# Attention's last units and the entry to the experts: rows turned later, both early gathers together, last logits on VectorE, last x on ScalarE, third expert's rows gathered early

## Chip, cores and metric

The kernel runs on one core of a Trainium2 chip. The metric is device time in microseconds (us) of one launch. Engines are named as in the profile: PE (TensorE matmul), DVE (VectorE), ACT (ScalarE), POOL (GpSimd), SP (SyncE, which here issues loads and stores).

## The reference

Attention without softmax, a norm, then a mixture of experts in which each row goes to one expert or to none:

```python
kv = np.einsum('bhsd,bhse->bhde', k, v)          # B=8, H=8, S=576, D=64
out = np.einsum('bhsd,bhde->bhse', q, kv)
rms = np.sqrt(np.mean(out * out, axis=-1, keepdims=True) + 1e-06)
attn = out / rms * g_norm
x = attn.transpose(0, 2, 1, 3).reshape(4608, 512)
do_compute = x @ w_skip > 0                       # rows that get an expert
logits = x[do_compute] @ w_gate                   # 8 experts
e_idx = np.argmax(logits, axis=1)
gate_w = softmax(logits)[range(len(logits)), e_idx]
h = np.maximum(x[rows_of_e] @ w1[e], 0.0)         # 512 -> 1024
y[rows_of_e] = gate_w * (h @ w2[e])               # 1024 -> 512
out = x;  out[do_compute] = x[do_compute] + y
```

## The kernel before

**Order.** The order of the program text is the order on each engine: it is written by hand. Attention is cut into 36 units n = 0 to 35 (NU = 36), each of 128 positions of two tiles and half the heads; the units of one tile pair are a couple, u = 0 and u = 1. The last couple, 34 and 35, holds the positions that don't fill a tile (i is None) of several batches.

**One turn of the attention loop** (L951 to L984), for n from 0 to 37: PE turns q of unit n+1; ACT takes the square root for n-1 (root, L525); jobs booked as "early"; PE multiplies q by the state (values, L496, or L504 for units 34 and 35) and ACT squares the product (L510); jobs "mid"; DVE sums the squares (squares, L518; from n = 30 ahead of norm) and for n-1 takes the reciprocal (L532) and multiplies the PSUM product by it into xl (norm, L537, 128x584: per head 64 values of x and 9 partial logits, eight experts and the skip score); jobs "pe"; POOL adds the partial logits (finish: lp L554 for each unit, lp+lp L558 and lg L562 for each couple); jobs "dve"; jobs "end". The product with g that makes x itself (xb, L567, on POOL) is kept in a list and issued one unit later by scale(), behind that unit's reciprocal; from the couple's second xb a store to the output follows. Units 30 and 33 hold their product in the PSUM tile sum_ps, all others in one of two tiles o_ps.

**The choice of experts** goes in three groups, when units 12, 22 and 36 are done (ends). choose (L608 to L634, DVE): mx, sh, oh, fi, fi, ohb, of which ohb marks each row's expert. rank (PE, L645 to L651): counts the rows of each expert up to every row. number (DVE, L662 to L677): turns the counts into a place for each row, lo_i and hi_k, and the one-hot oha. hits and weighed (L690 ohc, L698 bv) and place (PE, L710) then bring each row's number to its place: settle is place for a group of tiles.

**The early start.** After the second group, early() (L842 to L883) finds expert 0's first 192 rows from what is known by then: a small one-hot, place (L869), rows (L873), row and src (L859, L861), then a POOL gather of 128 rows (L863) and, booked as a job of the same turn, put_more: a matmul (L879), row and src, a gather of 64 rows. first_in(0) and first_in(1) turn the gathered rows on PE (L801) and ACT copies them to xt_first (L828, L830); first_layer_1 (L814) makes the first IN = 2 of the FC = 8 slices of layer 1, ACT their relu into ht_first (L817).

**At n = 36**: DVE makes ohc of the known groups (128x528), then choose of the last group; scale(NU, chosen[-1]) issues the last three xb (units 33, 34, 35) behind ohb; then bv for the known groups (L698).

**Entry to the experts** (L1484 to L1507, quoted in the diff). layer_1 makes slices of layer 1 for expert 0's first rows (L1112, relu on ACT L1114 into ht0), layer_2 slices of layer 2 for one piece of them (L1124), again_rows and slot_rows (L1051) the tables of row numbers (src, asrc for reading, rows, arows for writing), gather_all(r) the gathers of expert r (L1084, on POOL), gates() the softmax weights, expert_in turns gathered rows (L1093, ACT copies to xt). Expert 0's remaining rows then go through layer 1 (L1112 on xt). From expert 1 on the products are done in the fast form of L1192, with ACT copying intermediate sums p and u (L1202) and DVE adding (L1196). In experts(), gather_all(2) stands in the turn of r = 0 (L1423), and later experts' gathers two turns ahead. The results are scaled on DVE (L1336) and scattered to the output by POOL (L1339).

Of the kernel before, what the change touches and what calls it, by code (L numbers as in the profile page):

```python
# [8 lines left out]
FP32 = mybir.dt.float32  # L9
# [3 lines left out]
ALU = mybir.AluOpType  # L13
# [4 lines left out]
def kernel(  # L18
# [423 lines left out]
    def at(step, part, job):  # L442
        todo.setdefault((step, part), []).append(job)
# [84 lines left out]
    def norm(n):  # L528

        nq, b, i, u = units[n]  # L530
        (ps, _), rs = ops.pop(n), rss.pop(n)
        inverse = nc.vector.reciprocal(out=rs[:, :, :], in_=rs[:, :, :])  # L532
        if n < NU - 2:
            scale(n, inverse)
        r4 = rs[:, :, :].unsqueeze(3)
        xl = att_pool.tile([P, 2, 2, PK], FP32, tag="xl", name="xl", bufs=4)
        nc.vector.tensor_tensor(  # L537
            out=xl[:, :, :, :].rearrange("p x y (a k) -> p x (y a) k", a=2),
            in0=ps[:, :, 0:2 * PK].rearrange("p x (h k) -> p x h k", k=KD),
            in1=r4.to_broadcast([P, 2, 4, KD]), op=ALU.mult)  # L540
        return lambda: finish(n, xl)

    def finish(n, xl):
        nq, b, i, u = units[n]
        g = sum(2 * nq >= x for x in ends)
        t0 = 2 * nq - ([0] + ends)[g]
        if t0 == 0 and u == 0:
# [8 lines left out]
        if u == 1:  # L556
            del halves[nq]
            nc.gpsimd.tensor_tensor(out=lp[:, 0, :, :, :], in0=lp[:, 0, :, :, :],  # L558
                                    in1=lp[:, 1, :, :, :], op=ALU.add)
            both = lp[:, 0, :, :, :] if i is not None else \  # L560
                lp[:, 0, :, :, :].rearrange("p r w g -> p w r g")
            nc.gpsimd.tensor_tensor(out=lgs[g][:, t0:t0 + 2, :], in0=both[:, 0, :, :],  # L562
                                    in1=both[:, 1, :, :], op=ALU.add)
        if u == 0:
            xbs[nq] = xb_pool.tile([P, 2, DM], FP32, tag="xb", name="xb")
# [242 lines left out]
    def first_layer_1():  # L808

        hps = ps_q.tile([P, 512], FP32, tag="q", name="q_ps")  # L810
        for f in range(IN):
            cols = slice(f * KEPT, (f + 1) * KEPT)
            for dc in range(DC):
                nc.tensor.matmul(out=hps[:, cols], lhsT=w_sb[0][0][:, dc, f * P:(f + 1) * P],  # L814
                                 rhs=xt_first[:, dc, :], start=(dc == 0), stop=(dc == DC - 1),
                                 skip_group_check=True)
        at(NU, "early", lambda: nc.scalar.activation(  # L817
            out=ht_first[:, :, :], in_=hps[:, 0:IN * KEPT].rearrange("p (f t) -> p f t", f=IN),
# [20 lines left out]
    assert ends[LAST - 1] == 4 * (KNOWN // S) + 2  # L839
    NE = ends[LAST - 1]  # L840

    def early():  # L842
# [24 lines left out]
        def put():  # L867
            for t in range(NE):
                nc.tensor.matmul(out=ps, lhsT=oha_k[:, t, :],  # L869
                                 rhs=bv[:, t, :, :].rearrange("p c i -> p (c i)"), start=(t == 0),  # L870
                                 stop=(t == NE - 1), skip_group_check=True)
            rows = gat_pool.tile([P, 2], FP32, tag="rows1", name="rows1")
            nc.vector.tensor_reduce(out=rows[:, :], in_=ps.rearrange("p (c i) -> p c i", i=2),  # L873
# [3 lines left out]
            def put_more():  # L877
# [3 lines left out]
                gather(more, 64, P)  # L881
            at(now[0], "pe", put_more)
        yield "mid", put  # L883
# [62 lines left out]
    for part in range(2):  # L946
        at(NU - 3 + 2 * part, "early", lambda part=part: first_in(part))
    at(NU - 1, "end", first_layer_1)

    PACE = (2, 4)  # L950
    for n in range(NU + 2):  # L951
# [17 lines left out]
        if n == NU:  # L969
            ohc = hits(0, NE, colid_i, gat_pool, NE)  # L970
            drain(choose(LAST))
            scale(NU, chosen[-1])
            first_bv = weighed(ohc, 0, NE, row_k, 2, gat_pool, NE)
        jobs(n, "dve")
# [16 lines left out]
    with tc.tile_pool(name="wpool_b", bufs=1, reuse_waits="tile") as wpool_b, \  # L991
# [391 lines left out]
        def experts(pieces, widths, srcs, xt, ht, yps0, tables, group):  # L1383

            for r in range(E):
# [36 lines left out]
                if r == 0:  # L1422
                    gather_all(2, pieces, *srcs)  # L1423
                    ys = [bank() for _ in todo]
# [82 lines left out]
        load_ahead(0, landed)  # L1507
# [73 lines left out]
```

## Time and profile before

| | us |
|---|---|
| three runs | 380.49, 382.15, 384.62 (median 382.15) |
| the profiled execution | 381.18 |
| its span, first to last instruction | 379.4 |
| TensorE clock granted, mean | 0.997 of full |

The profile is one execution, cut into instructions by engine. A row of a timeline gives start, duration, engine, line, operation, out<-in with the shape, the count, and in brackets how long the engine had been idle and what ended that. A row of the waits gives the total, the count and the longest. Of the places named above:

| what | line, engine | first start, us | duration, us |
|---|---|---|---|
| gathers of the first rows, 128 and 64 | L863 POOL | 107.39, 109.98 | 1.08, 1.01 |
| turning the first 128 rows | L801 PE | 111.43 | 0.63 |
| values of 33, 34, 35 | L496, L504 PE | 111.89, 112.99, 115.53 | 1.17, 0.74, 0.74 |
| first slices of layer 1 | L814 PE | 116.72 | 2.9 |
| xl of 34, 35 | L537 DVE | 118.12, 119.13 | 0.77 each |
| last logits lg | L562 POOL | 121.04 | 0.22 |
| ohc of the known groups | L690 DVE | 119.82 | 0.70 |
| rank | L645 PE | 123.32 | 0.7 |
| last three xb | L567 POOL | 123.09 | 5.27 together |
| gathers of experts 0 and 1 | L1084 POOL | 134.86 to 141.44 | about 1 each |
| expert 0's remaining rows, layer 1 | L1112 PE | 142.78 | 4.3, twice |
| scatters of expert 0's rows | L1339 POOL | 154.07, 155.40 | about 1 each |
| gathers of expert 2 | L1084 POOL | 163.15, 164.45, 165.73 | about 1 each |

### The profile page before, as it was taken

The page shows a single profiled execution, that of the slowest core. Times are in us where ns is not written, and L with a number is a line of the kernel's source. Part 1 is how long each engine was busy: PE and PEld are TensorE (multiplying, and loading weights), DVE is VectorE, ACT ScalarE, POOL GpSimd, SP SyncE. Part 2 cuts the span into 40 slices and gives each one's busy share as a digit, 9 for nine tenths or more (in the row PEclk, how much of TensorE's full clock was granted, in tenths as well). Part 3 has the DMA queues.
Part 4 walks back from the last instruction along what each step waited for, and adds up shares of the span by engine and source line. Part 5 has one row for each costly group of instructions (what it writes and reads, how often), then busy time and mean ns, then how long its engine had stood idle before and what let it go on. Part 6 is the DMA issues. An engine that isn't in the chain of part 4 may idle for free.

```text
span 379.4 us, 9624 instructions
## 1 busy us (share of the span) xinstructions
PE 363.5 (96%) x3848; PEld 312.1 (82%) x3848; DVE 244.9 (65%) x626; ACT 142.4 (38%) x383; POOL 124.9 (33%) x195
## 2 busy tenths in 40 slices
PE   8999999999988999989999999999999999999994
PEld 4688797898877759669879987988988988998983
DVE  3355457767878861846757656875876876877831
ACT  2466575766763302214402420430440430431410
POOL 7036467555677560234113303212202211202003
PEclk9999999999999999999999999999999999999998
DMA  8999999995669639945716362772662762700001
GB/s 288 394 391 387 402 402 400 404 372 196 189 242 262 184 98 323 387 145 199 250 39 218 127 224 59 244 269 51 235 226 70 263 197 95 269 3 28 29 1 53
DMA packets 32039, 81.70 MB, mean 215 GB/s; under 512 B 2474, under 2 KB 2482, under 8 KB 31988
## 3 DMA queue, kind: packets, MB, share of 16 engines
q1 hardware_dynamic: 28176, 69.47, 52.2%
q0 software_dynamic: 3792, 11.53, 9.1%
q8 instruction: 32, 0.52, 0.6%
q14 instruction: 19, 0.16, 0.1%
q10 hardware_dynamic: 20, 0.02, 0.1%
HBM read 66.80 MB, written 14.48 MB: 214 GB/s over the span
## 4 chain that ended last, share of the span: by engine, by line
PE 81%; issue 9%; ACT 3%; DVE 3%; POOL 2%; DMA 1%; POOLq 0%; DVEq 0%; ACTq 0%
PE bank L1192 44%; PE bank L1124 7%; PE o_ps L496 6%; PE sum_ps L379 5%; PE bank L1112 4%; PE q_ps L460 3%; PE g_ps L393 2%; PE bank L1093 2%; PE q_ps L170 2%; DMA xg<-out_dram,src 1%; DVE rs L518 1%; DVE xl L537 1%; ACT sq L510 1%; PE q_ps L814 1%; PE g_ps L411 1%
## 5 line engine op out<-in xcount | busy, mean ns | idle before, releaser
L1202 ACT COPY p<-bank 128x128 f32<-128x128 f32 (+6 forms) x70 | 20.8, 297 | 102.1 <-PE bank L1192 89.6
L1192 PE MATMUL bank<-xt,w 128*128 128x128 f32 (+5 forms) x336 | 55.5, 288 | 0.3 <-DVE bank L1196 0.3
L567 POOL TENSOR_TENSOR xb<-xl,g_b 128x512 f32<-128x512 f32 x36 | 44.4, 1235 | 32.3 <-DVE rs L532 30.4
L1192 PEld LDWEIGHTS bank<-xt,w 128*128 128x128 f32 x336 | 47.0, 190 | 2.2 <-DVE bank L1196 1.3
L1196 DVE TENSOR_TENSOR bank<-bank,p 128x128 f32<-128x128 f32 (+6 forms) x70 | 23.6, 337 | 37.1 <-PE bank L1192 35.5
L1192 PE MATMUL bank<-xs,s 128*128 128x128 f32 (+5 forms) x224 | 36.9, 289 | 1.6 <-ACT p L1202 1.6
L496 PE MATMUL o_ps<-kvd,qT 128*128 128x146 f32 x240 | 35.8, 290 | 1.0 <-ACT kvd L415 0.7
L1339 POOL DMA_INDIRECT out_dram<-xg,arows x9 | 10.6, 1174 | 74.4 <-DVE xg L1336 68.8
L1124 PE MATMUL bank<-w,ht 128*32 128x128 f32 (+2 forms) x436 | 34.5, 319 | 0.0
L518 DVE TENSOR_REDUCE rs<-sq 128x8 f32<-128x512 f32 x36 | 24.6, 682 | 15.1 <-ACT sq L510 14.9
L1192 PEld LDWEIGHTS bank<-xs,s 128*128 128x128 f32 x224 | 31.1, 190 | 2.7 <-ACT p L1202 2.6
L496 PEld LDWEIGHTS o_ps<-kvd,qT 128*128 128x128 f32 x240 | 31.6, 188 | 2.0 <-ACT kvd L415 1.5
L1339 POOL DMA_INDIRECT out_dram<-xg,rows x14 | 13.9, 994 | 55.6 <-DVE xg L1336 54.3
L1124 PEld LDWEIGHTS bank<-w,ht 128*32 128x32 f32 (+2 forms) x436 | 18.8, 120 | 13.2 <-issue 10.9
L537 DVE TENSOR_TENSOR xl<-o_ps,rs 128x584 f32<-128x584 f32 x34 | 26.1, 767 | 4.5 <-DVE rs L532 0.5
L1084 POOL DMA_INDIRECT xg<-out_dram,src x14 | 14.5, 1038 | 39.7 <-DMA out_dram<-xg,rows 13.4
L1192 PE MATMUL bank<-t,ht 128*128 128x256 f32 x112 | 27.1, 385 | 0.0
L1192 PE MATMUL bank<-w,ht 128*128 128x256 f32 x112 | 27.1, 384 | 0.0
L510 ACT ACTIVATE sq<-o_ps 128x512 f32<-128x512 f32 x34 | 20.3, 596 | 15.0 <-PE o_ps L496 14.4
L1192 PE MATMUL bank<-t,hs 128*128 128x256 f32 x112 | 25.3, 379 | 0.0
L379 PE MATMUL sum_ps<-v,k 64*64 64x64 f32 x1152 | 24.7, 223 | 0.4 <-issue 0.4
L379 PEld LDWEIGHTS sum_ps<-v,k 64*64 64x64 f32 x1152 | 20.8, 134 | 4.3 <-issue 1.9
(217 smaller groups left out, 679.5 us busy)
## 6 DMA issues: line engine op xcount, KB each, us to landing
w<-in_moe_w_dram SPq DMA_DIRECT2D x16, 2048.0 KB, 9.8
k<-in_k_dram SPq DMA_DIRECT2D x16, 576.0 KB, 9.9
v<-in_v_dram SPq DMA_DIRECT2D x16, 576.0 KB, 10.6
q<-in_q_dram SPq DMA_DIRECT2D x16, 576.0 KB, 11.2
out_dram<-xb SPq DMA_DIRECT2D x29, 256.0 KB, 8.9
out_dram<-xb POOLq DMA_DIRECT2D x7, 256.0 KB, 5.9
xg<-out_dram,src POOLq DMA_INDIRECT x16, 3.4
out_dram<-xg,rows POOLq DMA_INDIRECT x16, 6.9
```

The costliest lines, as they stand in the source:

```text
L379: nc.tensor.matmul(out=sum_ps[w * 64:(w + 1) * 64, a, u, :], lhsT=kt[r, 2 * u + w, c, :], rhs=vt[r, 2 * u + w, c, :], start=(c == 0), stop ...
L496: nc.tensor.matmul(out=ps[:, w, 0:2 * PK].rearrange("p (r k) -> p r k", r=2)[:, :, cols], lhsT=qT[:, w, a, :], rhs=kvds[b % KVD][:, u, w, ...
L510: nc.scalar.activation(out=sq[:, :, :, :], in_=heads(ps, G, G + 2 * D), func=ACT.Square)
L518: nc.vector.tensor_reduce(out=rs[:, :, :], in_=sq[:, :, :, :].rearrange("p x y (a d) -> p x (y a) d", a=2), axis=AX.X, op=ALU.add)
L537: nc.vector.tensor_tensor(out=xl[:, :, :, :].rearrange("p x y (a k) -> p x (y a) k", a=2), in0=ps[:, :, 0:2 * PK].rearrange("p x (h k) -> ...
L567: late.append((lambda: nc.gpsimd.tensor_tensor(out=xb[:, :, 4 * u * D:(4 * u + 4) * D].rearrange("p r (w x) -> p r w x", w=2), in0=xl[:, : ...
L1112: nc.tensor.matmul(out=hps[:, cols], lhsT=w_sb[r][0][:, dc, f * P:(f + 1) * P], rhs=xt[:, dc, cols], start=(dc == 0), stop=(dc == DC - 1))
L1124: nc.tensor.matmul(out=yps[q * m:(q + 1) * m, 0:n], lhsT=ht(f)[:, off:off + m], rhs=w_sb[r][1][:, f, q * n:(q + 1) * n], start=(f == 0), s ...
L1192: nc.tensor.matmul(out=out, lhsT=lhsT(i), rhs=rhs(i), start=start and i == 0, stop=i == k - 1, skip_group_check=True)
L1196: nc.vector.tensor_tensor(out=to, in0=x, in1=y, op=ALU.add)
L1202: nc.scalar.copy(out=t, in_=x)
L1339: ins = nc.gpsimd.indirect_dma_start(out=cut_rows(m)[:, :], out_offset=bass.IndirectOffsetOnAxis(ap=rows[:, col:col + 1], axis=0), in_=x, ...
```

## The change

1. first_in(0) moves from the "early" jobs of turn 33 (ahead of values(33)) to its "pe" jobs (behind it).
2. put_more runs directly after the first gather, so that the two gathers stand together on POOL. ohc of the known groups is made in early() rather than at n = 36.
3. For units 34 and 35, DVE makes no xl. last_logits multiplies only the logits' 36 + 36 columns by the reciprocal (two instructions a unit) and, after 35, one reduction over the eight heads gives lg; POOL's lp, lp, lp+lp and lg for this couple are gone. last_x: ACT makes x, 16 copies of 128x64 with the reciprocal as a scale. They are issued at n = 36, behind root(35), and the relu L817 behind them. The xb of 33 is issued one turn earlier (scale for n < NU-1); those of 34 and 35 wait for ACT, no longer for ohb.
4. At the entry, one slice of layer 1 (f = 2) stands ahead of rank instead of three; the others fill the places between the tables; layer 2's first slices come after them; all three experts' gathers (nine, before six) are issued together, and r = 0 issues none.

```diff
@@ norm, finish
-        if n < NU - 2:
+        if n < NU - 1:
             scale(n, inverse)
         r4 = rs[:, :, :].unsqueeze(3)
         xl = att_pool.tile([P, 2, 2, PK], FP32, tag="xl", name="xl", bufs=4)
+        if n >= NU - 2:
+            last_logits(n, ps, rs)
+            last_x.append(lambda: norm_by_scalar(n, ps, rs, xl))
+            return None
...
+    def last_logits(n, ps, rs):
+        nq, b, i, u = units[n]
+        if u == 0:
+            halves[nq] = att_pool.tile([P, 2, G, 8], FP32, tag="le", name="le", bufs=1)
+        le = halves[nq]
+        for a in range(2):
+            nc.vector.tensor_tensor(
+                out=le[:, :, :, 4 * u + a:4 * u + a + 3:2].rearrange("p r g w -> p r w g"),
+                in0=ends_of(heads(ps, 0, PK))[:, :, :, a, :],
+                in1=rs[:, :, a:a + 3:2].unsqueeze(3).to_broadcast([P, 2, 2, G]), op=ALU.mult)
+        if u == 1:
+            g, t0 = place_of_logits(nq)
+            nc.vector.tensor_reduce(out=lgs[g][:, t0:t0 + 2, :], in_=halves.pop(nq)[:, :, :, :],
+                                    axis=AX.X, op=ALU.add)
+
+    def norm_by_scalar(n, ps, rs, xl):
+        for r in range(2):
+            for h in range(4):
+                w, a = divmod(h, 2)
+                cols = slice(G + a * D, G + (a + 1) * D)
+                nc.scalar.activation(out=xl[:, r, w, cols],
+                                     in_=heads(ps, cols.start, cols.stop)[:, r, w, :],
+                                     func=ACT.Copy, scale=rs[:, r, h:h + 1])
+        weigh(n, xl)
@@ first_layer_1
-        at(NU, "early", lambda: nc.scalar.activation(
+        at(NU, "dve", lambda: nc.scalar.activation(
@@ early
+            known_at.append(hits(0, NE, colid_i, gat_pool, NE))
             rows = gat_pool.tile([P, 2], FP32, tag="rows1", name="rows1")
...
-            at(now[0], "pe", put_more)
+            put_more()
@@ jobs
-        at(NU - 3 + 2 * part, "early", lambda part=part: first_in(part))
+        at(*((NU - 3, "pe"), (NU - 1, "early"))[part], lambda part=part: first_in(part))
@@ the loop
         if n == NU:
-            ohc = hits(0, NE, colid_i, gat_pool, NE)
+            for job in last_x:
+                job()
+            scale(NU)
             drain(choose(LAST))
-            scale(NU, chosen[-1])
-            first_bv = weighed(ohc, 0, NE, row_k, 2, gat_pool, NE)
+            first_bv = weighed(known_at[0], 0, NE, row_k, 2, gat_pool, NE)
@@ experts, r == 0
-                    gather_all(2, pieces, *srcs)
+                    if yps0 is None:
+                        gather_all(2, pieces, *srcs)
@@ entry
-        layer_1(0, xt_first, ht0, slice(0, KEPT), range(IN, 5))
+        layer_1(0, xt_first, ht0, slice(0, KEPT), range(IN, 3))
         rank(LAST)
         drain(number(LAST))
-        layer_1(0, xt_first, ht0, slice(0, KEPT), range(5, FC))
+        layer_1(0, xt_first, ht0, slice(0, KEPT), range(3, 4))
         settle(0, NE, first_bv)
         last_bv = columns(NE, NT - NE, colid_i, row_k, 2, gat_pool, NE)
-        y, y_more = [layer_2(0, ht_of, piece, None, range(IN)) for piece in first]
+        layer_1(0, xt_first, ht0, slice(0, KEPT), range(4, 7))
         settle(NE, NT, last_bv)
-        layer_2(0, ht_of, first[0], y, range(IN, 3))
+        layer_1(0, xt_first, ht0, slice(0, KEPT), range(7, FC))
         arows = slot_pool.tile([P, NRES], I32, tag="arows", name="arows")
         asrc = slot_pool.tile([P, NRES], I32, tag="asrc", name="asrc")
         again_rows(arows, asrc, range(0, SOON))
         rows, src = slot_rows(slice(0, NCOL), slot_pool, "")
-        layer_2(0, ht_of, first[0], y, range(3, 4))
+        y, y_more = [layer_2(0, ht_of, piece, None, range(IN)) for piece in first]
         again_rows(arows, asrc, range(SOON, len(runs)))
-        layer_2(0, ht_of, first[0], y, range(4, FC))
-        for r in range(2):
+        for r in range(3):
             gather_all(r, plan, src, asrc)
+        layer_2(0, ht_of, first[0], y, range(IN, FC))
         gates()
-        layer_2(0, ht_of, first[1], y_more, range(IN, 5))
         for piece in plan[0]:
             landed = expert_in(xg0, xt0, piece)
-        yps0 = [y, layer_2(0, ht_of, first[1], y_more, range(5, FC))]
+        yps0 = [y, layer_2(0, ht_of, first[1], y_more, range(IN, FC))]
         load_ahead(0, landed)
```

More of the change, by code (lines that the diff above doesn't have):

```diff
@@ L541, in norm, with place_of_logits @@
         return lambda: finish(n, xl)
+    last_x = []
+    def place_of_logits(nq):
+        g = sum(2 * nq >= x for x in ends)
+        return g, 2 * nq - ([0] + ends)[g]
+    def last_logits(n, ps, rs):
+        nq, b, i, u = units[n]
+        assert i is None
+        if u == 0:
[19 more added lines that the diff above has]
+        weigh(n, xl)
     def finish(n, xl):
         nq, b, i, u = units[n]
-        g = sum(2 * nq >= x for x in ends)
-        t0 = 2 * nq - ([0] + ends)[g]
+        g, t0 = place_of_logits(nq)
         if t0 == 0 and u == 0:
@@ L563, in finish, with weigh @@
                                     in1=both[:, 1, :, :], op=ALU.add)
+        weigh(n, xl)
+    def weigh(n, xl):
+        nq, b, i, u = units[n]
         if u == 0:
@@ L840 @@
     NE = ends[LAST - 1]
+    known_at = []
     def early():
```

## The prediction

> **What bounds the kernel now.** I read the busy table first, then the waits of TensorE (PE) alone, then the timelines of the four engines around the change. The page gives PE 96% of the span:
>
> ```profile
> PE 363.5 (96%) x3848; PEld 312.1 (82%) x3848; DVE 244.9 (65%) x626; ACT 142.4 (38%) x383; POOL 124.9 (33%) x195
> ```
>
> So an edit pays only if it closes one of PE's gaps, and costs if it opens one. The waits of PE, from 90 us to the end, are few (line waited at, what it waited for, us):
>
> ```profile
> PE bank L1192 <- ACT p L1202: 1.6, 1, 1.6
> PE o_ps L504 <- DVE xl L537: 1.4, 1, 1.4
> PE q_ps L801 <- DMA xg<-out_dram,src: 1.2, 1, 1.2
> PE bank L1112 <- issue: 0.6, 1, 0.6
> PE q_ps L814 <- ACT xt_first L830: 0.4, 1, 0.4
> PE g_ps L879 <- DVE rows L873: 0.3, 1, 0.3
> ```
>
> They sum to 5.5 us, all between 105 and 168 us: that is the whole prize. The three that the edits aim at are the gather wait at 111.43 (L801, first rows), the xl wait at 115.53 (L504, unit 35), and the 1.56 us at 167.16 (L1192), which coincides with the third expert's gathers (163.15 to 166.73). After 168 us PE never waits a tenth of a microsecond that this view lists.
>
> The hand-over from attention to experts is on VectorE (DVE) and GpSimd (POOL):
>
> ```profile
> 121.30 0.27 DVE L614 TENSOR_REDUCE mx<-lg 128x14 f32<-128x112 f32 x1 [0.78 <-POOL lg L562]
> ...
> 122.73 0.27 DVE L634 TENSOR_TENSOR ohb<-eorder,fi 128x112 bf16<-128x112 f32 x1
> ```
>
> The last logits come from POOL at 121.26, the choice of experts (mx to ohb) takes 1.7 us, and PE's rank needs ohb at 123.0. PE doesn't notice: three slices of layer 1 lie ahead of rank and run until 123.3.
>
> ```profile
> 119.42 4.06 PE L1112 MATMUL bank<-xt_first,w 128*128 128x192 f32 x24
> ```
>
> **What the Trainium skill says.** "SBUF — State Buffer", section "Who interferes with whom": a DVE instruction with two SBUF inputs and a POOL instruction that reads SBUF exclude each other for a whole instruction; reductions and operations with a PSUM input don't. The trace agrees: src (L861) takes 0.86 us beside an xb (other times 0.16), each oha (L677) 2.03 beside the last xb, and those xb, 1.18 alone, take 2.13 and 2.03. "ScalarE: Activation LUTs", section "What ACT_TABLE_LOAD costs", gives an activation about 186 ns + 0.833 ns an element, some 93 ns more for a scale that is a pointer, about 93 ns of which overlaps the next: 64 elements come every 0.24 us, 0.33 without overlap. The trace before has no such form; its nearest (L525, 8 elements) takes 0.30.
>
> **Part 1, first rows turned after values(33).** Four transposes move behind values(33); nothing is added. The 1.16 us wait at L801 goes, but values(33) then waits for what is late next: its PSUM, which the xl of unit 30 reads until 111.29. It starts at about 111.4 instead of 111.89: **0.5 us** earlier, and so the chain behind it (square, squares, root, xl, values(35), L814). The copy to xt_first, on ScalarE (ACT), now lies behind the square of 33; first rows are needed only at L814, four microseconds later.
>
> **Part 2, both early gathers at once; ohc moved.** Same instructions; on POOL the second gather passes one xb (1.18 us), which is later by the gather's 1.3. POOL works without a gap from 111.0 to 120.2, so its backlog ends where it did: lg of unit 33 at 119.56. The 0.70 us ohc goes from the choice to just ahead of rows (L873), where DVE waits 0.85 us for PE's place (L869) as it is: hidden, at worst 0.7 later. The second row and src come before the squares of 31 instead of behind them; DVE waits for PE's L879 some 0.3 there, and gets it back, since src no longer lies beside an xb (0.86 to 0.16). Gain or loss on PE 0, up to 0.7 lost if unit 30's xl slips.
>
> **Part 3, last logits on DVE, last x on ACT.** DVE loses two xl (2 x 0.77) and gains four products of 36 elements (0.2 each, between L773's 0.18 and L617's 0.27) and one reduction (0.27): -1.54 + 0.8 + 0.27 = -0.5 us. POOL loses lp, lp, lp+lp, lg (0.25 + 0.65 + 0.26 + 0.22 = 1.4 us). ACT gains 16 scaled copies: 16 x 0.24 = 3.8 us, 5.3 at 0.33. They begin behind root(35), 117.92 + 0.30 less the 0.5 of part 1 = 117.7; so unit 34's x is there at 119.6 to 120.4, unit 35's at 121.5 to 123.0. The relu L817 and layer 1's relus queue behind; the first reader of their results on PE is layer 2, eight microseconds on.
>
> The last logits are then done on DVE at about 118.8. But mx reads unit 33's logits too, which POOL ends at 119.56: mx starts at 119.6, not 121.3, **1.7 us earlier**. Now the catch. Before, the last three xb were held behind ohb. After, the xb of 33 follows lg(33) at once (119.6 to 120.7), and those of 34 and 35 as soon as ACT delivers. They take turns with the choice, whose sh, oh, second fi and ohb each read two SBUF inputs: sh waits to 120.7 and ends at 121.0; xb(34) to 122.2; oh to 122.5; the first fi, a reduction, beside xb(35), which holds to 123.7; then second fi (0.2) and ohb (0.3): **ohb at 124.2**. If ACT needs 0.33 a copy, xb(35) comes after ohb, which is then at 123.3. With no exclusion at all: 119.6 + 1.7 = 121.3. I take **124.0**, with 121.3 and 124.2 for the range. Behind it, oha no longer meets an xb: 2 x 1.3 instead of 4.03.
>
> **Part 4, entry to the experts.** Only one slice of layer 1 is left ahead of rank. PE: L814 at 116.2 (116.72 - 0.5), 2.7 us for it, 1.3 for f=2: at rank by 120.2. It waits for ohb: 0.2 us to start behind it, so 124.0 + 0.2 - 120.2 = **4.0 us idle**, where before it was none. From there to the first product on expert_in's rows, PE has the same work as before: the stretch from 116.72 to 142.14 (142.78 less its 0.64 of idle) is 25.4, less the 4.0 already done, 21.4. So 124.2 + 21.4 = 145.6, against 142.78: **+2.8 us** (121.3: 142.9, +0.1). Within it, VectorE must not come late: last_bv at 130.9 before, 7.9 behind ohb, now 1.4 sooner thanks to oha, so 6.5; PE gets to it after rank 0.7, f=3 to 6 5.2 and a settle 0.7 = 6.6. Just in time; a miss costs some tenths.
>
> The third expert's three gathers join the first six on POOL (nine at 1.33 us: about 135.6 to 147.5), and the scatters of expert 0's rows, at 154.07 before, follow. PE waits for none of it: the first six are ahead in the queue as before, and layer 2 of the second piece covers their copies.
>
> The stall at 167.16: PE waited for p from ACT, which was itself released only at 166.80, as the r=2 gathers ended; the weight load of SP moved at 166.69 too. The 0.64 at 142.78 coincides with the first six gathers in the same way. Coincidence is all the trace shows. I take it as caused by the gathers being issued there: **-1.6 us**. If not: 0.
>
> **Sum**, against the profiled execution's own time, 381.18 us (span 379.4 and 1.8 around it): +2.8 - 1.6 = +1.2, so 382.4. The part 1 gain is inside the +2.8, since PE waits for ohb whatever it had saved. That execution lies 1.0 below the median of the runs, 382.15; their spread is 4.1. I put the time at **382.6**.
>
> **Rivals.**
> 1. *Forecast*: xb takes turns with the choice, rank waits 3 to 4 us, the late stall goes: +0.3 to +1.4; 381.5 to 383. For it: the exclusion seen at L861, L677 and L567. Chance 0.40.
> 2. *The choice slips through*: mx goes at 119.6 and POOL's xb lose the race or come late; ohb 121.3 to 122.5. L1112 on xt at 142.9 to 144.1, +0.1 to +1.3, less 1.6: -1.5 to -0.3; 379.5 to 381.5. For it: before, bv went ahead of a waiting xb at 122.93. Against: xb(33) is already running when sh comes. Chance 0.27.
> 3. *Slower: PE's wait for ohb at rank, with nothing given back.* Place: rank (L645), from 120.2. Price: 2.8 us on the path at ohb 124.0, 3.0 at 124.2, with the stall at 167 staying (its cause isn't the gathers, or it moves with them). It decides from ohb later than 121.2 if the stall stays, than 122.8 if it goes. 384 to 384.3; to 385.5 if last_bv and the row tables, behind the same ohb, come a further 1.4 late (the time that oha was to save). For it: PE's last gaps are small and the new one is 4 us. Against: oha is freed. Chance 0.25.
> 4. *It doesn't do what it says*: ACT's copies come so late, or the roots behind them, that POOL's and DVE's order shifts and mx still waits to 121. Then ohb at 122.7 to 123, PE idle 2.7, +1.5, less 1.6: 381. Chance 0.08, shared by both sides.
>
> **How the numbers follow.** Case 1 is likeliest; 2 gives the lower end and 3 the upper. The range, **379.5 to 385.5**, holds cases 1, 2 and most of 3. A measurement of this kernel tells about 1%, 3.8 us, from no change, and no case comes to that but the end of 3 with a mishap added: faster by over 1% 0.04 (nearly the whole prize of 5.5 won), within 1% 0.84, slower by over 1% 0.12.
>
> **What would show it.** In the profile after: mx waiting for lg of unit 33 at about 119.6; sh, oh or fi stretched to 1 us or starting behind an xb's end; PE idle before rank (L645) for <- DVE ohb, 3 to 4 us; oha 1.3; L801 without a wait; L1192 <- ACT p gone. I am wrong if rank waits under 1.5 us (case 2), if the wait at L1192 stays (case 3), or if PE waits for p or weights anywhere after 168 us.

## The result, and the profile after

The changed kernel takes 383.88 us (median of 22 runs, 383.18 to 385.29); the kernel before, in the same job, 383.19 us (22 runs, 380.49 to 385.37). The ratio is 1.0027, 95% interval 1.0011 to 1.0043: slower by 0.4 to 1.6 us. The forecast was 382.6 from a median of 382.15, in a range of 379.5 to 385.5.

The profiled execution of the changed kernel has a span of 382.8 us. Its lines are numbered some 40 higher than before: L504 to L541, L614 to L656, L645 to L687, L814 to L856, L1112 to L1157, L1192 to L1237 are the pairs that matter. Place (L869, now L912), the last step on PE ahead of what the change moves, starts at 106.79 us instead of 105.70, so **1.09 us of the difference in span lies ahead of the change** and is taken off wherever a start is compared below. This lead goes with the execution, not with the kernel. Of the 14 profiles of this document, six record TensorE at full clock, to stay, from 4.2 to 5.5 us, and in these place starts at 105.70 to 106.25 us; the other eight record it from 9.3 to 10.9 us, and there place starts at 106.41 to 107.32. Both groups hold kernels with and without the change's parts.

The page's row of PE, and then its waits from 90 us to the end, after (total, times, longest):

```profile
PE 366.9 (96%) x3848; PEld 314.9 (82%) x3848; DVE 244.0 (64%) x629; ACT 145.4 (38%) x399; POOL 120.8 (32%) x191
```
```profile
PE g_ps L690 <- DVE ohb L676: 2.7, 1, 2.7
PE sum_ps L496 <- ACT sq L510: 0.8, 1, 0.8
PE o_ps L504 <- DVE xl L541: 0.8, 1, 0.8
PE q_ps L856 <- ACT xt_first L872: 0.4, 1, 0.4
PE bank L1157 <- issue: 0.4, 1, 0.4
...
PE bank L1237 <- ACT p L1247: 0.2, 1, 0.2
```

PE is busy 3.4 us longer with the same 3848 products (1.3 of it ahead of place, 2.1 between place and the first fast product), and has no less idle time. The gather wait (1.2) is gone, but 0.8 of it comes back one product later, ahead of values(33); the xl wait fell from 1.4 to 0.8. The 1.6 us wait for p at the third group of fast products (L1192) is gone too: the 0.2 that is listed stands elsewhere, at 206.81 us. The same products before and after:

```profile
167.16 0.85 PE L1192 MATMUL bank<-xs,s 128*128 128x172 f32 x4 [1.56 <-ACT p L1202]
```
```profile
169.62 1.41 PE L1237 MATMUL bank<-xs,s 128*128 128x172 f32 x8
```

The largest wait is new, at rank, for ohb. The timeline of VectorE, before and after, shows how ohb became late: mx starts earlier, but three of the instructions behind it take three to four times as long.

```profile
121.60 0.27 DVE L617 TENSOR_TENSOR sh_k<-lg,mx 128x112 f32<-128x112 f32 x1
121.91 0.27 DVE L622 SCALAR_TENSOR_TENSOR oh<-sh_k,eorder 128x112 f32<-128x112 f32 x1
...
122.52 0.18 DVE L630 SCALAR_TENSOR_TENSOR fi<-lg,fi 128x14 f32<-128x14 f32 x1
```
```profile
120.58 0.27 DVE L656 TENSOR_REDUCE mx<-lg 128x14 f32<-128x112 f32 x1 [0.68 <-POOL lg L599]
120.89 0.93 DVE L659 TENSOR_TENSOR sh_k<-lg,mx 128x112 f32<-128x112 f32 x1
121.86 1.14 DVE L664 SCALAR_TENSOR_TENSOR oh<-sh_k,eorder 128x112 f32<-128x112 f32 x1
123.03 0.27 DVE L669 TENSOR_REDUCE fi<-oh 128x14 f32<-128x112 f32 x1
123.33 0.73 DVE L672 SCALAR_TENSOR_TENSOR fi<-lg,fi 128x14 f32<-128x14 f32 x1
124.10 0.27 DVE L676 TENSOR_TENSOR ohb<-eorder,fi 128x112 bf16<-128x112 f32 x1
...
126.28 2.10 DVE L719 TENSOR_TENSOR oha_k<-row_i,lo_i 128x896 bf16<-128x896 int32 x2
```

On POOL, at the same time, the last three xb, and on ACT the copies that feed them:

```profile
120.51 3.53 POOL L609 TENSOR_TENSOR xb<-xl,g_b 128x512 f32<-128x512 f32 x3
```
```profile
119.15 3.38 ACT L576 ACTIVATE xl<-o_ps,rs 128x64 f32<-128x64 f32 x16 [0.30 <-DVE rs L532]
```

The xb run back to back, 1.18 us each, ending at about 121.7, 122.9 and 124.0; sh, oh and fi end at 121.82, 123.00 and 124.06, each just behind one of these ends. The two reductions, mx and the first fi, keep their 0.27. And PE, behind its wait, is slow for a while:

```profile
121.36 0.38 PE L687 MATMUL g_ps<-top,ident 128*128 128x120 f32 x2
124.43 0.21 PE L690 MATMUL g_ps<-ohb,ut 128*128 128x112 bf16 x1 [2.69 <-DVE ohb L676]
...
124.93 2.25 PE L1157 MATMUL bank<-xt_first,w 128*128 128x192 f32 x8
126.97 1.09 PE L752 MATMUL g_ps<-bv,oha_k 128*128 128x48 bf16 x22
```

Eight products of this shape take about 1.5 us elsewhere. The table by stretches says why; its columns are the stretch, its length, busy time and count of PE, PEld, DVE, ACT and POOL, then the granted clock, the DMA share and GB/s:

```profile
125.00:126.00 1.00, 1.00 (x9) 1.00 (x6) 1.00 (x4) 0.00 (x0) 0.00 (x0) 0.81 1.00 406
126.00:127.00 1.00, 1.00 (x5) 0.83 (x5) 0.97 (x4) 0.00 (x0) 0.00 (x0) 0.50 1.02 410
...
128.00:129.00 1.00, 1.00 (x6) 1.00 (x5) 0.97 (x4) 0.00 (x0) 0.00 (x0) 0.50 0.36 127
129.00:130.00 1.00, 1.00 (x8) 1.00 (x8) 0.95 (x2) 0.00 (x0) 0.00 (x0) 0.99 0.02 8
```

For 3.4 us, from 125.6 to 129, TensorE has half its clock. The forecast didn't have this; when it comes is worked out in the last section.

### The profile page after: what moved, and what is told of

The parts are those of the page before. It is cut to its first block, busy times and chain, and to the rows that moved or that the text cites. A ratio compares the mean times of both kernels' runs of the same rounds, so it can differ in the third digit from the quotient of the medians.

```text
span 382.8 us, 9644 instructions
## 1 busy us (share of the span) xinstructions
PE 366.9 (96%) x3848; PEld 314.9 (82%) x3848; DVE 244.0 (64%) x629; ACT 145.4 (38%) x399; POOL 120.8 (32%) x191
## 4 chain that ended last, share of the span: by engine, by line
PE 82%; issue 6%; POOL 4%; DVE 3%; ACT 3%; POOLq 0%; ACTq 0%; DVEq 0%
PE bank L1237 44%; PE bank L1169 9%; PE o_ps L496 6%; PE sum_ps L379 5%; PE bank L1157 4%; PE q_ps L460 3%; POOL xb L609 2%; PE g_ps L393 2%; PE q_ps L170 2%; PE bank L1138 2%; PE g_ps L1096 1%; PE g_ps L411 1%; PE g_ps L752 1%; ACT qT L463 1%; DVE xl L541 1%
## 5 line engine op out<-in xcount | busy, mean ns | idle before, releaser
L1237 PE MATMUL bank<-xt,w 128*128 128x128 f32 (+5 forms) x336 | 55.5, 288 | 0.4 <-DVE bank L1241 0.3
L609 POOL TENSOR_TENSOR xb<-xl,g_b 128x512 f32<-128x512 f32 x36 | 42.7, 1187 | 30.3 <-DVE rs L532 30.3
L1237 PEld LDWEIGHTS bank<-xt,w 128*128 128x128 f32 x336 | 47.0, 190 | 2.3 <-DVE bank L1241 1.5
L1237 PE MATMUL bank<-xs,s 128*128 128x128 f32 (+5 forms) x224 | 36.8, 288 | 0.2 <-ACT p L1247 0.2
L1237 PEld LDWEIGHTS bank<-xs,s 128*128 128x128 f32 x224 | 31.1, 190 | 1.3 <-ACT p L1247 1.2
L541 DVE TENSOR_TENSOR xl<-o_ps,rs 128x584 f32<-128x584 f32 x32 | 24.5, 767 | 4.3 <-DVE rs L532 0.5
L1237 PE MATMUL bank<-t,ht 128*128 128x256 f32 x112 | 27.1, 385 | 0.0
L1237 PE MATMUL bank<-w,ht 128*128 128x256 f32 x112 | 27.1, 384 | 0.0
L1237 PE MATMUL bank<-t,hs 128*128 128x256 f32 x112 | 25.3, 379 | 0.0
```

Of the source, the lines that this page charges most:

```text
L541: nc.vector.tensor_tensor(out=xl[:, :, :, :].rearrange("p x y (a k) -> p x (y a) k", a=2), in0=ps[:, :, 0:2 * PK].rearrange("p x (h k) -> ...
L609: late.append((lambda: nc.gpsimd.tensor_tensor(out=xb[:, :, 4 * u * D:(4 * u + 4) * D].rearrange("p r (w x) -> p r w x", w=2), in0=xl[:, : ...
L1237: nc.tensor.matmul(out=out, lhsT=lhsT(i), rhs=rhs(i), start=start and i == 0, stop=i == k - 1, skip_group_check=True)
```

## The experiments

Two readings of each profile carry most of what follows: **A**, from place to the first fast product (L1192, L1237), which holds attention's end and the entry, and **B**, from there to the end of the span. Rank's start is that of its second product (L690), the first that needs ohb, counted from place. "Half clock" says whether and where the granted clock falls to 0.5 between 100 us and the end of the work. Ratios are to the runs of before in the same job; the jobs ran on different chips, so ratios of different jobs are compared with care. The names "gathers alone" and "best" stand for the kernels of experiment 7.

| kernel | ratio (95%) | A | B | rank from place | half clock |
|---|---|---|---|---|---|
| before | 1 | 58.46 | 215.24 | 17.83 | no |
| before, second profile | 0.9995 (0.9965 to 1.0025) | 60.24 | 215.77 | 19.63 | 117 to 121 |
| changed | 1.0027 (1.0011 to 1.0043) | 62.15 | 213.86 | 17.64 | 125 to 129 |
| changed, again | 1.0076 (1.0054 to 1.0098) | 61.50 | 213.43 | 17.63 | 125 to 129 |
| third rows late | 1.0049 (1.0027 to 1.0072) | 59.93 | 215.15 | 17.62 | no |
| first rows early | 1.0068 (1.0040 to 1.0096) | 59.95 | 213.44 | 17.66 | no |
| wait filled | 1.0016 (1.0000 to 1.0032) | 60.80 | 213.63 | 17.64 | no |
| no slice ahead | 1.0146 (1.0120 to 1.0172) | 62.91 | 213.44 | 17.63 | 125 to 129 |
| last xb held | 0.9984 (0.9970 to 0.9999) | 59.57 | 213.51 | 15.58 | no |
| entry as before | 0.9959 (0.9944 to 0.9975) | 58.86 | 213.52 | 17.64 | no |
| entry as before, again | 0.9937 (0.9918 to 0.9956) | 59.23 | 213.94 | 17.64 | no |
| gathers alone | 0.9997 (0.9979 to 1.0015) | 59.33 | 213.16 | 19.42 | 117 to 121 |
| gathers alone, again | 0.9963 (0.9943 to 0.9983) | 61.02 | 213.48 | 19.50 | 118 to 122 |
| best | 0.9931 (0.9913 to 0.9950) | 58.82 | 213.77 | 17.34 | no |

**1. The entry's order put back.** The order of work on PE behind attention is that of before; the gathers stay together.

```diff
-        layer_1(0, xt_first, ht0, slice(0, KEPT), range(IN, 3))
+        layer_1(0, xt_first, ht0, slice(0, KEPT), range(IN, 5))
         rank(LAST)
         drain(number(LAST))
-        layer_1(0, xt_first, ht0, slice(0, KEPT), range(3, 4))
+        layer_1(0, xt_first, ht0, slice(0, KEPT), range(5, FC))
         settle(0, NE, first_bv)
...
```

> The changed kernel with the entry's order of before (three slices of layer 1 ahead of rank, layer 2's first slices between the two settles), the nine gathers still together. Theory (PE's 2.7 us of waiting at rank for ohb, and the half clock of TensorE from 125 to 129 us that follows it, are what the change costs): the wait at rank falls from 2.7 to about 0.4 us, the granted clock stays 1.00 at 125 to 129, rank starts within 0.2 us of where it does in the changed kernel, the first product on expert 0's remaining rows starts 3.3 to 3.9 us earlier, and the time is 380 to 381 us, ratio to before 0.990 to 0.995. Rival (the wait is hidden or only moves behind VectorE's tables): ratio stays at 1.001 to 1.004.

The timeline of PE in this run:

```profile
120.58 4.06 PE L1157 MATMUL bank<-xt_first,w 128*128 128x192 f32 x24
...
124.96 0.21 PE L690 MATMUL g_ps<-ohb,ut 128*128 128x112 bf16 x1
```

Rank starts 17.64 us behind place, as in the changed kernel, but PE has done two more slices by then: no wait for ohb is listed, the clock stays full, A falls by 3.3 us. The time is 380.95 us, ratio 0.9959, just outside the expected 0.990 to 0.995, but far from the rival's 1.001 to 1.004. So of the parts that had been changed together, the order at the entry is the one that costs; the rest together is a gain.

**2. The wait filled with useless work.** This parts the wait from the clock.

```diff
+        spare = bank()
+        for f in (2, 3):
+            for dc in range(DC):
+                nc.tensor.matmul(out=spare[:, 0:KEPT], lhsT=w_sb[0][0][:, dc, f * P:(f + 1) * P],
+                                 rhs=xt_first[:, dc, :], start=(dc == 0), stop=(dc == DC - 1))
         rank(LAST)
```

> The changed kernel with two idle slices of layer 1 (16 products into a bank that nobody reads, 2.6 us) ahead of rank: PE works while it waits, and gets nothing for it. It parts the wait from the clock. If the half clock comes from PE's idling: the clock stays 1.00 at 125 to 129, rank starts when it does in the changed kernel (0.2 later at most), and the time falls by the 1.5 to 1.8 us that the half clock cost: 382 to 382.5, ratio 0.997 to 0.9995. If the half clock has another cause: it stays, ratio 1.002 to 1.005.

```profile
121.04 2.76 PE L1534 MATMUL bank<-xt_first,w 128*128 128x192 f32 x16
123.64 0.38 PE L687 MATMUL g_ps<-top,ident 128*128 128x120 f32 x2
124.11 0.21 PE L690 MATMUL g_ps<-ohb,ut 128*128 128x112 bf16 x1
...
124.61 1.55 PE L1157 MATMUL bank<-xt_first,w 128*128 128x192 f32 x8
```

Rank doesn't move (17.64), the clock stays full, the next eight products take 1.55 us, not 2.25. From rank to the first product on expert 0's remaining rows it is 20.93 us (124.11 to 145.04), against 22.50 in the changed kernel: **the half clock costs 1.57 us**. That the filled wait keeps the clock up is seen in more than this one profile: in this job 4 of its 22 runs have a mean clock of 0.995 or less, against 14 of the 15 of "third rows late" (experiment 4), which waits at rank. Such a mean counts a half clock anywhere in a run; the last section has a closer reason. The time, 382.89 us and 1.0016, missed its range, 0.997 to 0.9995, which had been worked out from a ratio of another job. The trace carries the 1.57 us, the median doesn't.

**3. The last xb held.** They wait for ohb as before the change.

```diff
-        if n < NU - 1:
+        if n < NU - 2:
             scale(n, inverse)
...
-            scale(NU)
             drain(choose(LAST))
+            scale(NU, chosen[-1])
```

> The changed kernel with the last three xb held behind ohb again, as before the change. Theory (POOL's xb stretch sh, oh and fi by 0.66 + 0.87 + 0.55 us): sh, oh, fi and ohb take 0.27, 0.27, 0.18 and 0.27; ohb ends 1.9 to 2.1 us earlier, rank waits 0.6 to 0.8 instead of 2.7, the clock stays full; but the xb then lie beside bv and oha, so that the columns of the last group come late and PE waits for them (about 1.3 us). Together -2 to -3 us: ratio 0.994 to 0.998. Rival (no exclusion; the choice is slow for another reason): rank waits 2.7 still, ratio 1.002 to 1.005.

The timelines of VectorE, PE and POOL:

```profile
120.04 0.28 DVE L659 TENSOR_TENSOR sh_k<-lg,mx 128x112 f32<-128x112 f32 x1
120.35 0.27 DVE L664 SCALAR_TENSOR_TENSOR oh<-sh_k,eorder 128x112 f32<-128x112 f32 x1
...
120.96 0.18 DVE L672 SCALAR_TENSOR_TENSOR fi<-lg,fi 128x14 f32<-128x14 f32 x1
...
123.72 4.02 DVE L719 TENSOR_TENSOR oha_k<-row_i,lo_i 128x896 bf16<-128x896 int32 x2
```
```profile
121.50 0.21 PE L690 MATMUL g_ps<-ohb,ut 128*128 128x112 bf16 x1 [0.64 <-DVE ohb L676]
...
129.41 0.51 PE L752 MATMUL g_ps<-bv,oha_k 128*128 128x48 bf16 x14 [1.33 <-DVE bv L740]
```
```profile
121.52 5.27 POOL L609 TENSOR_TENSOR xb<-xl,g_b 128x512 f32<-128x512 f32 x3 [1.82 <-DVE ohb L676]
```

Same instructions, same operands, only the three xb elsewhere: sh, oh and fi fall by 0.65, 0.87 and 0.55 us, rank comes 2.06 us earlier. The exclusion that "SBUF — State Buffer" in the Trainium skill states under "Who interferes with whom" is thereby shown for this place, with its other half: oha, now beside the xb, goes from 2.10 back to 4.02 us, and the last columns make PE wait 1.33, as expected. The exclusion isn't avoided, only moved. The ratio, 0.9984, is just above the expected 0.994 to 0.998.

**4. The third expert's gathers put back.**

```diff
-                    if yps0 is None:
-                        gather_all(2, pieces, *srcs)
+                    gather_all(2, pieces, *srcs)
...
-        for r in range(3):
+        for r in range(2):
             gather_all(r, plan, src, asrc)
```

> The changed kernel with the third expert's gathers back in the turn of expert 0. If it was the gathers' place that made PE wait for p at the first fast product: that wait (0.2 us now) is 1.5 to 1.8 again, and the time 1.2 to 1.6 us longer, ratio 1.005 to 1.008. If not: 1.001 to 1.004.

```profile
124.84 0.21 PE L690 MATMUL g_ps<-ohb,ut 128*128 128x112 bf16 x1 [2.69 <-DVE ohb L676]
...
125.34 1.55 PE L1157 MATMUL bank<-xt_first,w 128*128 128x192 f32 x8
...
169.69 0.85 PE L1237 MATMUL bank<-xs,s 128*128 128x172 f32 x4 [1.11 <-issue]
```

The wait behind the first fast product is back, at the same products as before the change, with 1.1 us instead of the 1.5 to 1.8 expected and put down to "issue"; the ratio, 1.0049, is just below the expected 1.005. Column B of the table tells more: in the three profiles with the gathers late it is 215.15 to 215.77 us, in the eleven with the gathers early 213.16 to 213.94. On the means, 215.4 and 213.6, **the gathers' place is worth 1.8 us** in B. The cleanest pair is this profile and that of "first rows early" (experiment 5), alike in rank and both without a half clock: A and B together are 275.08 and 273.39, 1.7 us apart. Some of it may come back in A: near the gathers PE has waits of 0.4 to 1.1 us together in six of the eleven, against 0.6 in both profiles of before. The first two lines show something else: the same 2.69 us of wait, and no half clock behind it.

**5. The changed kernel again, and first rows early.** These ask how regular the half clock is, and what part 1 is worth.

> The changed kernel once more, as a partner for the others of this job and for a second look at TensorE's clock. Its first profile shows the clock at half from 125 to 129 us behind a wait of 2.7 us at rank; the run with the third gathers late shows the same wait and no half clock. If the half clock follows some executions only: about even odds of seeing it here; without it the stretch from rank to the first product on expert 0's remaining rows takes 20.9 us instead of 22.5. Ratio 1.001 to 1.004.

The half clock is here again, at the same place: from rank to the remaining rows 22.50 us (124.40 to 146.90). The ratio, 1.0076, missed its range, and its interval (1.0054 to 1.0098) lies wholly above that of the first measurement (1.0011 to 1.0043). On this job's chip the change costs 2.9 us (383.01 against 380.09) rather than 0.7; why is open.

```diff
-        at(*((NU - 3, "pe"), (NU - 1, "early"))[part], lambda part=part: first_in(part))
+        at(NU - 3 + 2 * part, "early", lambda part=part: first_in(part))
```

> The changed kernel with part 1 undone: the first rows are turned ahead of values(33) again. If what PE gains there is swallowed by the wait for ohb, since POOL's backlog and not PE sets when the choice begins: L501's stretch starts 0.4 to 0.5 us later, the wait at rank is shorter by as much (2.2 instead of 2.7), rank starts at the same time, and the time is that of the changed kernel within 0.15%. If part 1 carries a gain: the time is 0.4 to 0.5 us longer and rank later by as much.

("L501's stretch" is a slip; the first slices of layer 1, L856, are meant.)

```profile
124.77 0.21 PE L690 MATMUL g_ps<-ohb,ut 128*128 128x112 bf16 x1 [2.53 <-DVE ohb L676]
```

L856 starts 10.74 us behind place instead of 10.57, only 0.17 later where 0.4 to 0.5 was expected, since the gathers land sooner than before the change anyway; the wait is 0.16 shorter, and rank is where it was (17.66 against 17.64). Its ratio, 1.0068, can't be told from 1.0076. Behind a wait that VectorE ends, part 1 is worth nothing.

**6. No slice ahead of rank.**

```diff
-        layer_1(0, xt_first, ht0, slice(0, KEPT), range(IN, 3))
         rank(LAST)
         drain(number(LAST))
-        layer_1(0, xt_first, ht0, slice(0, KEPT), range(3, 4))
+        layer_1(0, xt_first, ht0, slice(0, KEPT), range(IN, 4))
```

> The changed kernel with the last slice (f = 2) moved behind rank as well: PE has nothing ahead of rank, and waits there 4.0 us instead of 2.7, for the same ohb. Theory (the work ahead of rank is what covers the choice): rank starts at the same time, all behind it comes 1.3 us later, and the longer wait brings the half clock surely, so its profile shows it and the time is 1.3 to 2.5 us above the changed kernel's: ratio 1.005 to 1.010. Rival (the slack behind rank, at VectorE's tables, takes the slice up): ratio 1.001 to 1.004.

```profile
123.88 0.21 PE L690 MATMUL g_ps<-ohb,ut 128*128 128x112 bf16 x1 [3.99 <-DVE ohb L676]
...
124.38 4.53 PE L1157 MATMUL bank<-xt_first,w 128*128 128x192 f32 x16
```

The wait is 3.99 us, rank stays at 17.63, A is 1.4 longer than in the second profile of the changed kernel: the slice's own 1.3 and little else, the half clock being in both. The median is 2.9 us longer (385.87 against 383.01, five and six runs), and the ratio, 1.0146, lies above the expected 1.005 to 1.010. The mean clock granted in three of the five runs is 0.984 to 0.989, in the profiled one 0.993, so those had more half-clock time than the profile shows; where it lay isn't recorded.

**7. The gathers alone, on the kernel before,** in two jobs, the second time beside the full set of parts; **the kernel before once more;** and **the best version.**

```diff
-                    gather_all(2, pieces, *srcs)
+                    if yps0 is None:
+                        gather_all(2, pieces, *srcs)
...
-        for r in range(2):
+        for r in range(3):
             gather_all(r, plan, src, asrc)
```

> The kernel before with one edit: the third expert's gathers join the first six. If their place made PE wait for p at the first fast product: that wait falls from 1.6 to 0.2 us, nothing else changes, and the time falls 1.1 to 1.5 us, ratio 0.996 to 0.997: most of what the best version so far gains (0.996). If that version's gain comes from the attention parts: ratio 0.998 to 1.000 here.

The median doesn't move: 380.25 against 380.09, which is what was expected if the gathers were worth nothing. B is short here too (213.16), but A holds a half clock, from 117 to 121 us, behind the waits at attention's end that the first profile of before has as well, without it. That job's chip ran the kernel before 2 to 3.5 us faster than the others, and no profile of before was taken there.

> The kernel before, as a partner for the others of this job and for a second profile of it. Ratio 0.998 to 1.002. Open is whether the two waits of its first profile that coincide with gathers (0.64 us ahead of expert 0's remaining rows, 1.56 us at the first fast product) come in every execution: if so both are here again, within 0.3 us; if not, the change's early gathers took away less than the 1.6 us that the prediction counted.

The second profile of before shows what the first didn't. A row of the timeline of PE, and one of its waits:

```profile
117.02 4.55 PE L814 MATMUL q_ps<-xt_first,w 128*128 128x192 f32 x16 [0.44 <-ACT xt_first L830]
```
```profile
PE bank L1192 <- ACT p L1202: 2.4, 1, 2.4
```

L814 takes 4.55 us instead of 2.87, at half the clock; the wait for p is 2.4 instead of 1.6, the other one (0.6) as before. The kernel before, too, loses clock behind its idle time, and the profile that the forecast was made from happened to be one without.

> The kernel before with the third expert's gathers joined to the first six, again, in one job with the version that also has the attention parts. If the gathers' place is worth what the first profile of before says: 0.996 to 0.997. If it is worth little on most executions: 0.998 to 1.001, and the waits of the second profile of before are shorter than those of the first.

> The changed kernel with the entry's order of before, again, on the same chip as the kernel with the gathers alone. What it has beyond that one is parts 1 to 3 (first rows later, logits on VectorE, x on ScalarE, xb of the last units early). PE starts on expert 0's first slices 0.4 us earlier and is held by no wait at rank, so 0.3 to 0.6 us less than the gathers alone, plus what half-clock stretches it is spared: ratio 0.994 to 0.998. If parts 1 to 3 are worth nothing: the same as the gathers alone within 0.1%.

In one job: gathers alone 381.87 us (0.9963), gathers and parts 1 to 3 381.09 (0.9937). The gathers alone are worth 1.7 us here (383.60 for before), as in B and as expected, and nothing in the other job; what parts 1 to 3 add, 0.8 us, lies within the intervals, which overlap. Parts 2 and 3 weren't measured one by one. The best version starts from the second of these:

```diff
-        if n < NU - 1:
+        if n < NU - 2:
             scale(n, inverse)
...
-        at(*((NU - 3, "pe"), (NU - 1, "early"))[part], lambda part=part: first_in(part))
+        at(*((NU - 3, "pe"), (NU - 2, "end"))[part], lambda part=part: first_in(part))
...
-        if THIRD + 2 <= n < NU:
+        if THIRD + 2 <= n < NU and n != NU - 3:
             squares(n)
...
-        if n < THIRD + 2:
+        if n < THIRD + 2 or n == NU - 3:
             squares(n)
...
-            scale(NU)
             drain(choose(LAST))
+            scale(NU, chosen[-1])
```

> As the one before, with three edits: the last three xb behind ohb again; in turn 33 VectorE makes unit 32's xl before it sums the squares of 33 (the root that xl needs is there 1.0 us earlier than it is used); ACT's copy of the second part of the first rows goes ahead of unit 34's root. PE's waits ahead of values(35) and of the first slices (0.8 and 0.4 us) fall below 0.3 together, ohb comes 1.9 us earlier so that rank isn't reached too soon, and the time is 0.6 to 0.9 us below entry_as_before_again: ratio 0.992 to 0.996. If the freed time is swallowed behind it (the columns of the last group, 4.0 us of oha beside xb): the same as entry_as_before_again within 0.1%.

```profile
114.89 0.74 PE L504 MATMUL o_ps<-kvd,q 64*64 64x73 f32 x32
116.39 2.87 PE L856 MATMUL q_ps<-xt_first,w 128*128 128x192 f32 x16 [0.75 <-ACT xt_first L872]
```

The wait ahead of values(35), 0.8 us, is gone; 0.3 of it comes back ahead of the first slices (0.75 instead of 0.44, for ACT's copy), so the two didn't fall below 0.3 together. A is 0.4 us shorter than in its partner (58.82 against 59.23), the median 0.5 (380.55 against 381.09), within the intervals. Its ratio, 0.9931, is the lowest measured, but not told from its partner's.

## Why the prediction was right, and for which reasons

The sign and the mechanism came out, and so did the size in the first job: +0.45 us from median to median was forecast, +0.7 measured. That the sum fits is in part luck: two of its terms were wrong and cancelled in the profile, and the half clock, which it left out, burdens both kernels. Starts are in before's clock, that is, less the 1.09 us.

- **The prize**, 5.5 us, none of it behind 168 us: two rows of that view were passed over, 0.2 at 153.05 us and 0.3 at 306.02. Nothing hung on them.
- **Part 1**, values(33) at 111.4: measured 111.36, L856 at 116.27 (forecast 116.2). Right, and so is the wait for the xl of unit 30, which ends at 112.31 in the profile after, 0.14 ahead of values(33), though the view names ACT's sq, which ends with it; experiment 5 shows that only 0.17 us of it is the moved transposes, the rest comes with the gathers of part 2. Worth nothing while ohb is late.
- **Part 3**, mx at 119.6: 119.49. Right, as was what it waits for, lg of unit 33 on POOL. ACT's copies come every 0.21 us, under the 0.24 worked out from "ScalarE: Activation LUTs" of the Trainium skill, section "What ACT_TABLE_LOAD costs". oha, the two of them, take 2.10, less than the 2.6 counted.
- **ohb at 124.0**: it ends at 123.28. What failed here is the turn-taking: I let sh and oh each hold up the next xb by their own length (0.3 us), and counted fi's own 0.2 behind the last. POOL's xb run back to back all the same (3.53 us for three); VectorE's instruction finishes at the seam between two of them and costs POOL nothing. That makes ohb 0.7 early against the forecast.
- **Part 4**, PE reaching rank at 120.2: 120.27. Idle 4.0: 2.69, since the second product comes 3.07 behind and 0.38 of that is rank's first product; a little under the 3 to 4 that it named as a sign. From rank to the remaining rows 21.4: 20.93 at full clock (experiment 2), 22.50 with the half clock. **The missing term is the half clock, 1.57 us**; it stands against 0.9 us by which PE starts on rank sooner than forecast (123.34, not 124.2) and the 0.5 counted too much here, so the sum stayed as it was: the remaining rows at 145.84, forecast 145.6.
- **The late stall, -1.6**: -1.8 over all profiles (B). Right, and so is its cause, the gathers' place, which the forecast took from a coincidence. That it came out is again partly luck, since the wait differs from one profile of before to the other (1.56 and 2.42 us). Why a gather's issue holds up ACT's and PE's hand-overs remains open.
- **Rivals**: the forecast's own case held, by its difference of +0.3 to +1.4; its 381.5 to 383 us was missed because the median of three runs lay 1.0 below that of 22. Rival 3's mechanism (rank waits for ohb) was the same, without the stall given back. One sign of being wrong came, in small: behind 168 us PE waits 0.2 for p, at 206.81.

By the profile of the forecast the change should cost 2.3 us (A and B of the first rows: +3.69 - 1.38); by its second pair of profiles it gains 1.1 (+1.26 - 2.34). The medians say +0.7 in one job and +2.9 in the other. Part of the spread is how often the half clock comes. Of 66 runs of before in the last job 45 have a mean clock of 0.995 or less, and average 384.2 us, the other 21, at 0.997 and 0.998, 381.9; 21 of the 22 runs of the changed kernel in the first job have 0.995 or less; of the 22 of "entry as before" in the last job, 16 have 0.997 or more. So the change swaps a stretch of idling that often costs clock for one that mostly does. That the mean clock of these runs comes from the stretches seen in the profiles is an inference: only profiled executions show where the clock fell, and the mean also counts a half clock elsewhere (in the profile of "third rows late" from 7.50 to 10.91 us, and in all 14 for 0.3 to 3.4 us behind the last product). And the half clock doesn't explain the +2.9: in that job 12 of 20 runs of before have 0.993 or less too.

## What to carry to other kernels

Work laid ahead of a wait is the cover of the chain that ends it: before moving it behind the wait, date both ends, and then date them again with every engine that stretches that chain's instructions, as the xb do here, running at its earliest. An instruction "held behind" another may look like a needless wait and be what keeps a short critical chain clear. And an idle stretch of TensorE of two or three microseconds is to be priced at its length plus a possible 1.6 us of half clock behind it (1.57 measured); useless products in the gap avoid the second (experiment 2), useful ones both (experiment 1).

## What was not expected of the hardware

"TensorE: Matmul & The Clock Gate" of the Trainium skill says under "The HAM clock gate" that TensorE falls to half clock after an idle window of about 3.4 us, and that the windows run freely. The trace agrees with the second. In all 14 profiles the clock's changes lie whole multiples of 3.413 us apart; in the changed kernel full clock is first recorded at 9.56 us, and the changes at 125.62, 129.03 and 381.62 us come 34, 35 and 109 windows later. The first is too strict for this kernel: of PE's waits from 90 us on only one, of 3.99 us, is as long as 3.4. Stretches cut along these windows show what decides; the columns are as above, and PE's busy time, as the profile models it, stands behind the length. The changed kernel:

```profile
122.21:125.62 3.41, 1.19 (x19) 1.19 (x19) 3.31 (x6) 0.92 (x4) 1.95 (x3) 1.00 1.01 378
125.62:129.03 3.41, 3.41 (x32) 3.24 (x31) 3.34 (x10) 0.33 (x1) 0.00 (x0) 0.50 0.81 315
```

"Third rows late", with the same 2.69 us of wait, split between two windows:

```profile
120.14:123.55 3.41, 2.01 (x14) 1.85 (x13) 2.62 (x5) 3.41 (x16) 3.25 (x6) 1.00 0.95 283
123.55:126.97 3.42, 2.13 (x33) 2.06 (x33) 3.32 (x10) 0.04 (x1) 1.02 (x2) 1.00 1.04 410
126.97:130.38 3.41, 3.41 (x38) 3.41 (x35) 3.34 (x6) 0.83 (x3) 0.00 (x0) 1.00 0.57 217
```

The kernel before, its first profile and then its second, with waits of 1.44 and 0.44 us in both:

```profile
114.61:118.03 3.42, 2.05 (x40) 1.91 (x41) 3.03 (x6) 1.85 (x6) 3.26 (x7) 1.00 0.90 228
```
```profile
114.23:117.64 3.41, 1.53 (x38) 1.21 (x37) 3.03 (x7) 1.84 (x5) 3.25 (x7) 1.00 0.91 223
117.64:121.05 3.41, 3.41 (x12) 3.41 (x12) 2.91 (x6) 0.30 (x1) 2.88 (x8) 0.50 0.90 294
```

Between 20 and 370 us, the 14 profiles have six windows in which PE is busy for less than half (shares of 0.30 to 0.48), and each is followed by one at half clock; in all others PE is busy for 0.51 or more, and none is. (With the wait filled the lowest share is 0.73.) So what counts in these traces is a window less than half busy, and where the windows fall differs from one execution to the next: that is why the same program has the half clock in one profile and not in another. One window at the kernel's start doesn't fit ("third rows late", 4.08 to 7.50 us, 2.88 busy, half clock behind it), and stays unexplained.

From this an estimate, for one wait in work that is otherwise without gaps, if a window starts anywhere with the same chance: a wait of up to 1.7 us brings no half clock, one of 3.4 us or more always, and one between with a chance of about its length over 3.41 us, which for the 2.69 us at rank is 0.8. By it the 3.99 us without a slice ahead are sure to bring the half clock, and the order of before at the entry, where PE doesn't wait for ohb, is free of it there.
